# Low-rank attention with a gated feed-forward block: two early loads, the first batch's small pieces and one slot of batch 2 are moved

## The chip, the cores and the metric

The kernel runs on one core of a Trainium2 chip. The core has five engines that work side by side, each with its own queue of instructions taken in order: TensorE (PE in the profile, its weight loads PEld), VectorE (DVE), ScalarE (ACT), GpSimd (POOL) and SyncE (SP). Transfers are issued on the queues of SP, ACT and POOL and carried by 16 DMA engines that all of them share. TensorE reads SBUF and writes PSUM. Engines wait for one another on semaphores.

The metric is the device time of one execution in microseconds (us), less being better. It is given as the median of several runs.

## The reference

Part one is attention with keys and values that are projected from 1024 positions down to 64. There are 8 batches, 8 heads, 1024 positions and 64 elements per head. With E and F of 64 x 1024:

```
k_proj = E @ k          # per batch and head: 64 x 64
v_proj = F @ v
scores = (q @ k_proj.T) / 8
attn   = softmax(scores, over the 64 projected positions)
x      = attn @ v_proj  # heads side by side: 8192 tokens x 512
```

Part two is a gated feed-forward block on the 8192 tokens, with weights of 512 x 1536, 512 x 1536 and 1536 x 512:

```
g   = x @ w_gate
out = (g * sigmoid(g) * (x @ w_val)) @ w_out
```

## The kernel before, in words

Everything that TensorE multiplies is bf16. The weights stay in SBUF. The tokens are cut into 16 chunks (`c`) of 512: chunk c is half `ch` of batch `b`. For each chunk the feed-forward part goes over 12 blocks (`f`) of 128 columns. A block has a gate product (`f_g`, L367: four matmuls into a bank of PSUM called `gps`, then a tanh on ACT), a value product (`f_v`, L373: four matmuls into `vps`, then two operations on DVE that make the hidden tile `hT`), and a third of an output product of the chunk before (`f_y`, L386). These 192 blocks are the main loop. Every block t has two slots, 2t (between gate and value product) and 2t + 1 (after the output product), and the attention of later batches is laid into these slots by a table written out by hand (`place`, L426).

The attention of one batch has these pieces:

- `u_KV` (L140): k and v times E and F, giving the projected keys `ks` and values `BDV`. `u_V0` (L167) is the values' part for batch 0, a few head pairs at a time, with a copy by ACT.
- `u_KT` (L187): the projected keys transposed, and laid by four DVE copies into a block-diagonal operand `BD` for two positions at once.
- `u_T` (L211) transposes q on TensorE for chunks 0 and 1; `u_TD` (L226) has a DMA transpose do it for the others.
- `u_S` (L242): scores for one of eight units of a batch (chunk half, head group g, position pair i), four matmuls, then exp on ACT into `ee`. `u_R` (L263): row sums and reciprocals on DVE. `u_N` (L271): `ee` times the reciprocals, giving the bf16 attention tile `AA`.
- `u_A` (L289) transposes `AA` on TensorE, with a copy by DVE or ACT into `AT`; `u_AD` (L234) has a DMA transpose do it.
- `u_PV`, `u_PV2`, `u_PV1` (L305 to L343): attention times projected values, copied to `xT`, which is the operand of the feed-forward products.

For batches from 1 on, `u_S` of unit j stands in a slot `s0 + o + 3j`, `u_R` and `u_N` in the slot behind it, and the two `u_AD` four slots behind units 3 and 7. For batch 2, `o` is 13 and s0 is 48, so its first scores stand in slot 61, behind the output product of block 30. The transpose that they read, `u_TD(2, 0)`, is issued on SP in slot 57, once the load of q has landed.

The first half of chunk 0 has nothing to hide behind and is written out instruction by instruction (L459 to L570). The order of lines is the order of each engine's queue. ACT and SP issue the first loads: the first four heads of k in f32 (`kraw`, two loads, cast to bf16 by DVE and ACT), E and F. POOL makes the two identity matrices for transposes, then issues q, the other heads of k, v and the weights, which are cast to bf16 by the transfer itself. POOL can have eight loads under way; the ninth waits for the first to land. `warm` (L495) issues matmuls on zeros. `turn` transposes E and F. In the last lines, `f_mm` (L350) does the first half (256 tokens) of the products of blocks 0 and 1, between the pieces `u_A` and `u_PV2` that make the second half of `xT`; blocks 0 and 1 of the loop then do the second half, and from block 2 on the products have 512 tokens.

Of the kernel before, what the change touches and what calls it, by code (L numbers as in the profile page):

```python
# [22 lines left out]
P = 128  # L23
# [11 lines left out]
def kernel(  # L35
# [235 lines left out]
    def u_N(b, u):  # L271
        ch, w = divmod(u, 4)
        g, i = divmod(w, 2)
        if (b, ch) in BY_DMA:
            if (b, ch, "d") not in AA:
                AA[b, ch, "d"] = aw.tile([P, 4, H, KP], BF16, name="AAd", tag="AAd")
            a = AA[b, ch, "d"][:, 2 * i : 2 * i + 2, 4 * g : 4 * g + 4, :]
        else:
            a = AA[b, u] = aw.tile([P, 2, 4, KP], BF16, name="AA", tag="AA", bufs=4)
            a = a[:]  # L280
        eng = nc.vector if (b, u) == (0, 3) else nc.gpsimd
        eng.tensor_tensor(  # L282
            out=a.rearrange("p j h k -> p h j k"),
            in0=ee.pop((b, u))[:],
            in1=rr.pop((b, u))[:].unsqueeze(3).to_broadcast([P, 4, 2, KP]),
            op=ALU.mult,
        )
# [138 lines left out]
    def place(b):  # L426
        s0 = 48 * (b - 1)
        if b == 1:
            put(22, u_TD, 1, 0)
            put(29, u_KV, 1, "k")  # L430
            put(32, u_KT, 1)
            put(40, u_KV, 1, "v")
            sa = (35, 36, 37, 38, 41, 42, 43, 44)
            put(41, u_AD, 1, 0)
            put(30, u_TD, 1, 1)
            put(47, u_AD, 1, 1)
            sp = (44, 45, 46, 46, 66, 67, 68, 69)
        else:
            put(s0 + (8 if b == 2 else 0), u_KV, b)
            put(s0 + (11 if b == 2 else 3), u_KT, b)  # L440
            o = 13 if b == 2 else 6
            put(s0 + (9 if b == 2 else -6), u_TD, b, 0)
            put(s0 + (11 if b == 2 else -4), u_TD, b, 1)
            sa = [s0 + o + 3 * j for j in range(NJ)]
            put(sa[3] + 4, u_AD, b, 0)
            put(sa[7] + 4, u_AD, b, 1)
            sp = [s0 + i for i in (39, 41, 43, 45, 57, 59, 61, 63)]
        for j in range(NJ):
            put(sa[j], u_S, b, j)
            put(sa[j] + 1, u_R, b, j)  # L450
            put(sa[j] + 1, u_N, b, j)
        for i in range(8):
            put(sp[i], u_PV, b, i // 4, i % 4)
# [5 lines left out]
    with tc.manual_schedule():  # L459

        kb[0] = kv_pool.tile([P, H, NJ, D], BF16, name="kb", tag="kb")
        kraw = [aw.tile([P, 2, NJ * D], FP32, name="kraw", tag=tag) for tag in ("qTd", "AAd")]
        for i in range(2):
            nc.scalar.dma_start(
                out=kraw[i][:],
                in_=k[0, 2 * i : 2 * i + 2].rearrange("h (p j) d -> p h (j d)", j=NJ),
            )
        ef = []
        for which, src in (("E", E), ("F", F)):
            raw = const.tile([KP, S], FP32, name=f"{which}raw")  # L470
            (nc.sync if which == "E" else nc.scalar).dma_start(out=raw[:], in_=src)
            ef.append(raw)
        zeros = const.tile([P, CW], BF16, name="zeros")
        nc.vector.memset(zeros[:], 0.0)
        make_identity(nc, ident_fp[:])
        make_identity(nc, ident_bf[:])
        for i in range(2):
            nc.vector.memset(ks[i][64:P], 0.0)
            nc.vector.memset(BD[i][:], 0.0)
        nc.vector.memset(BDV[1][:], 0.0)  # L480

        def turn(which, at, halves=(0, 1)):
            for half in halves:
                ps = bank(at, [P, 4, KP], FP32, "efp")
                for i in range(4):
                    j = 4 * half + i
                    nc.tensor.transpose(
                        out=ps[:, i, :],
                        in_=ef[which][:, bass.ds(j, P, step=NJ)],
                        identity=ident_fp[:KP, :KP],  # L490
                    )
                js = slice(4 * half, 4 * half + 4)
                copy(nc.scalar, (ET, FT)[which][:, js, :], ps[:])

        def warm(n):  # L495

            ps = bank("v", [P, CW], FP32, "warm")
            for _ in range(n):
                nc.tensor.matmul(
                    out=ps[:], lhsT=zeros[:, 0:P], rhs=zeros[:],  # L500
                    start=True, stop=True,
                )


        dve, act = nc.vector, nc.scalar
        load_q(0, 0, (0, 2))
        load_k(0, 4, 8)
        load_q(0, 0, (2, 4))
        load_v(0, (0, 4, 6, 8))
        load_w_gv(0, 1)  # L510
        load_w_gv(1, 2, (0,))
        warm(11)
        turn(0, "v")
        warm(4)
        for h in range(4):
            for n in range(2):
                eng = act if (h, n) == (3, 1) else dve
                ds = slice(256 * n, 256 * (n + 1)) if h == 3 else slice(0, 512)
                if n == 0 or h == 3:
                    copy(eng, kb[0][:, h].rearrange("p j d -> p (j d)")[:, ds], kraw[h // 2][:, h % 2, ds])  # L520
        u_KV(0, "k", (0, 4), at="y")
        warm(1)
        u_T(0, 0, "a", act)
        u_KT(0, at="v", prs=(0, 2))
        u_T(0, 2, "a", act)
        turn(1, "a", (0,))
        u_S(0, 0, "g")
        u_R(0, 0)
        u_N(0, 0)
        load_w_gv(1, 2, (1,))  # L530
        warm(1)
        u_KV(0, "k", (4, 8), at="y")
        turn(1, "a", (1,))
        u_KT(0, at="v", prs=(2, 4))
        warm(1)
        u_T(0, 1, "a", act)
        u_A(0, 0, dve)
        u_T(0, 3, "a", dve)
        u_S(0, 2, "g")
        u_R(0, 2)  # L540
        u_N(0, 2)
        u_S(0, 1, "g")
        u_R(0, 1)
        u_N(0, 1)
        load_w_gv(2, 4)
        u_S(0, 3, "v")
        u_R(0, 3)
        u_V0(0, 2, "y")
        u_PV2(0, 0, 0, 0, act)
        warm(1)  # L550
        u_V0(2, 3, "y")
        u_A(0, 2, dve)
        u_PV1(0, 0, 2, 0, dve)
        u_V0(3, 4, "v")
        u_PV1(0, 0, 3, 0, act)
        u_N(0, 3)
        f_mm(0, 0, 0, 0)
        u_A(0, 1, act)
        u_A(0, 3, dve)
        f_mm(0, 0, 1, 0)  # L560
        u_PV2(0, 0, 0, 1, act)
        u_PV2(0, 0, 1, 1, dve)
        f_mm(0, 1, 0, 0)
        f_mm(0, 1, 1, 0)
        load_w_gv(4, 6)
        load_q(0, 1, hs=(0, 4))
        load_w_gv(6, 8)
        load_q(0, 1, hs=(4, 8))
        load_w_gv(8, 10)
        load_w_gv(10, 12)  # L570
        load_q(1, 0)
        load_k(1)
        load_wo(0)
        load_wo(1)

        for i, u in enumerate(range(4, 8)):
            put(11 + i, u_T, 0, u)
            put(13 + i, u_S, 0, u)
            put(14 + i, u_R, 0, u)
            put(14 + i, u_N, 0, u)  # L580
            put((17, 18, 20, 21)[i], u_A, 0, u, nc.scalar)
        put(19, u_PV, 0, 1, 0)
        put(20, u_PV, 0, 1, 1)
        put(22, u_PV, 0, 1, 2)
        put(22, u_PV, 0, 1, 3, nc.vector)
        put(20, load_v, 1)
        put(20, load_q, 1, 1)
        for b in range(1, B):
            place(b)
        for b in range(2, B):  # L590
            s0 = 48 * (b - 1) - (20 if b == 3 else 24)
            at = (43, 43, 44, 45) if b == 2 else (s0, s0 + 2, s0 + 4, s0 + 6)
            put(at[0], load_k, b)
            put(at[1], load_v, b)
            put(at[2], load_q, b, 0)
            put(at[3], load_q, b, 1)

        for s in slots:
            slots[s].sort(key=lambda x: x[0] not in (load_k, load_v, load_q))


        ypart = defaultdict(list)
        for c in range(B * CH - 1):
            for n in range(NFT):
                f = n if c else 4 + (2 * n + 1) // 3
                ypart[(c + 1) * NFT + f].append((c, n))

        for t in range(NIT):
            c, f = divmod(t, NFT)
            i = 1 if t < 2 else None  # L610
            f_g(c, f, i)
            run_slot(2 * t)
            f_v(c, f, i)
            for a in ypart.pop(t, ()):
                f_y(*a)
            run_slot(2 * t + 1)
        for n in range(9):
            f_y(B * CH - 1, n)
        f_y_last(B * CH - 1, 3)
        assert not slots and not ypart  # L620
# [29 lines left out]
```

The softmax here doesn't subtract the row's maximum and nothing guards it: scores larger than these inputs give would overflow.

## Time and profile before

| | us |
|---|---|
| time, median of 4 runs | 569.94 (569.52 to 570.31) |
| profiled execution: its time | 570.12 |
| profiled execution: its span | 568.3 |
| TensorE busy | 557.7 (98%) |
| DVE, ACT, POOL busy | 340.3, 235.6, 110.0 |
| q of chunk 0, first half: issued, landed | 1.77, 9.57 |
| kraw, second half: landed, first cast | 7.35, 7.40 |
| k, heads 4 to 7: landed, first matmul | 11.83, 11.92 |
| first gate matmul | 20.39 |
| first gate product with 512 tokens | 25.50 |
| S of batch 2, unit 0 | 105.07 |

The profile is of one execution. A line of its timeline has the start, the duration (or, for several merged instructions, the time that they cover), the engine, the source line, the operation with output and inputs, the shape, and in brackets how long the engine had stood idle and what released it. L138 is the line of a copy helper, so its groups are told apart by the tile they write. Busy time of TensorE is modelled at the end of each matmul; the starts of neighbouring matmuls tell more of its pace. A DMA view lists the queues: q0 is POOL's, q10 ACT's and q1 SP's in this run, with the packets, the MB and the share of the 16 engines' time. Bytes of q0 are counted as written (bf16), half of what it reads.

### The profile page before, as it was taken

What the parts mean: (1) busy time and instruction counts of PE and PEld (TensorE: products, weight loads), DVE (VectorE), ACT (ScalarE), POOL (GpSimd) and SP (SyncE); (2) the same over time, 40 slices, a digit from 0 to 9 for tenths busy, and PEclk for the clock granted to TensorE, in tenths of its full rate; (3) what the DMA queues carried; (4) which work ended last, traced back from release to release, by engine and by line L of the source; (5) the groups of instructions that cost most, each with busy time, mean ns of one, the idle gap of its engine ahead of it and who ended that gap; (6) DMA issues with size and microseconds to landing.
All of it is one profiled execution on the core that took longest, in us unless ns stands there. A gap on an engine that the chain in (4) does not pass through costs nothing.

```text
span 568.3 us, 7876 instructions
## 1 busy us (share of the span) xinstructions
PE 557.7 (98%) x2911; PEld 266.4 (47%) x2966; DVE 340.3 (60%) x580; ACT 235.6 (41%) x413; POOL 110.0 (19%) x123
## 2 busy tenths in 40 slices
PE   8899999999999999999999999999999999999997
PEld 4554444444444444444444444444444444444444
DVE  4686764766376654766466655666547665545550
ACT  3464442453435433443434434354343542443222
POOL 6751250124002400124002230023100220000000
PEclk9999999999999999999999999999999999999999
DMA  9999999729902696129930499105990214101012
GB/s 205 178 198 186 178 142 201 139 59 200 199 26 73 107 199 122 37 57 157 187 83 37 76 180 197 50 18 105 195 182 20 59 36 74 38 37 37 20 39 92
DMA packets 111159, 62.91 MB, mean 111 GB/s; under 512 B 64272, under 2 KB 102416, under 8 KB 111120
## 3 DMA queue, kind: packets, MB, share of 16 engines
q0 software_dynamic: 42816, 29.36, 35.9%
q1 hardware_dynamic: 67392, 31.46, 26.8%
q10 hardware_dynamic: 912, 1.57, 0.9%
q8 instruction: 23, 0.38, 0.3%
q14 instruction: 16, 0.13, 0.1%
HBM read 60.29 MB, written 16.78 MB: 136 GB/s over the span
## 4 chain that ended last, share of the span: by engine, by line
PE 94%; DMA 3%; ACT 1%; issue 1%; DVE 0%; POOL 0%; POOLq 0%
PE gps L358 29%; PE vps L358 29%; PE yps L396 28%; PE kvp L150 3%; PE sc L251 3%; PE pv L309 2%; DMA qb<-in_q_dram 1%; DMA qTd<-qb 1%; PE aTp L298 0%; ACT ee L255 0%; PE qTp L217 0%; ACT th L370 0%; POOL AA L282 0%; PE pv L324 0%; PE kTp L194 0%
## 5 line engine op out<-in xcount | busy, mean ns | idle before, releaser
L377 DVE SCALAR_TENSOR_TENSOR s<-th,gps 128x512 f32<-128x512 f32 x192 | 130.5, 680 | 135.6 <-ACT th L370 135.2
L358 PE MATMUL gps<-xT,wg 128*128 128x512 bf16 (+1 forms) x756 | 195.6, 377 | 1.3
L358 PE MATMUL vps<-xT,wv 128*128 128x512 bf16 (+1 forms) x763 | 196.2, 377 | 0.7
L396 PE MATMUL yps<-wo,hT 128*128 128x512 bf16 (+2 forms) x759 | 191.3, 376 | 0.8
L370 ACT ACTIVATE th<-gps 128x512 f32<-128x512 f32 x192 | 114.7, 597 | 155.6 <-PE gps L358 145.7
L382 DVE TENSOR_TENSOR hT<-s,vps 128x512 bf16<-128x512 f32 x192 | 132.0, 688 | 20.7 <-DVE s L377 0.9
L282 POOL TENSOR_TENSOR AAd<-ee,rr 128x512 bf16<-128x512 f32 x56 | 58.3, 1042 | 343.0 <-issue 156.4
L396 PEld LDWEIGHTS <-hT 128*128 128x128 bf16 x780 | 76.2, 98 | 89.9
L358 PEld LDWEIGHTS <-wv 128*128 128x128 bf16 x776 | 74.0, 98 | 83.2 <-issue 2.9
L358 PEld LDWEIGHTS <-wg 128*128 128x128 bf16 x776 | 74.1, 98 | 81.1 <-issue 1.0
L406 ACT ACTIVATE ysb<-yps 128x512 f32<-128x512 f32 (+1 forms) x65 | 38.4, 591 | 76.7 <-PE yps L396 71.3
L138 ACT CAST xT<-pv 128x512 bf16<-128x512 f32 (+1 forms) x62 | 35.9, 581 | 51.8 <-PE pv L309 50.5
L266 DVE TENSOR_REDUCE zz<-ee 128x8 f32<-128x512 f32 x64 | 43.5, 679 | 21.4 <-ACT ee L255 21.4
L255 ACT ACTIVATE ee<-sc 128x512 f32<-128x512 f32 x64 | 37.9, 595 | 24.8 <-PE sc L251 23.6
L251 PEld LDWEIGHTS <-qTd 128*128 128x128 bf16 x224 | 17.1, 98 | 13.9 <-DMA qTd<-qb 0.9
L309 PE MATMUL pv<-AT,BDV 128*128 128x512 bf16 x60 | 22.4, 379 | 0.2
L251 PE MATMUL sc<-BD,qTd 128*128 128x128 bf16 x224 | 21.7, 219 | 0.5 <-DMA qTd<-qb 0.4
L268 DVE RECIPROCAL rr<-zz 128x8 f32<-128x8 f32 x64 | 13.0, 203 | 6.3
L108 POOL DMA_DIRECT2D qb<-in_q_dram x18 | 16.3, 906 | 0.6 <-DMA qb<-in_q_dram 0.6
L150 PE MATMUL kvp<-kb,ET 128*64 128x512 bf16 (+1 forms) x72 | 15.5, 358 | 0.0
L162 DVE CAST BDV<-kvp 64x256 bf16<-64x256 f32 x7 | 3.0, 426 | 19.9 <-ACT ks L158 17.8
L150 PE MATMUL kvp<-vb,FT 128*64 128x512 bf16 x56 | 13.4, 382 | 0.0
(59 smaller groups left out, 136.4 us busy)
## 6 DMA issues: line engine op xcount, KB each, us to landing
out_dram<-ysb SPq DMA_DIRECT2D x63, 256.0 KB, 2.3
qb<-in_q_dram POOLq DMA_DIRECT2D x14, 512.0 KB, 18.1
kb<-in_k_dram POOLq DMA_DIRECT2D x7, 1024.0 KB, 11.4
vb<-in_v_dram POOLq DMA_DIRECT2D x7, 1024.0 KB, 13.9
wo<-in_moe_w_out_dram POOLq DMA_DIRECT2D x2, 768.0 KB, 22.2
wg<-in_moe_w_gate_dram POOLq DMA_DIRECT2D x5, 256.0 KB, 8.1
wv<-in_moe_w_val_dram POOLq DMA_DIRECT2D x5, 256.0 KB, 8.7
kraw<-in_k_dram ACTq DMA_DIRECT2D x2, 512.0 KB, 5.0
```

The source lines that it names most:

```text
L138: (nc.scalar.copy if eng is nc.scalar else eng.tensor_copy)(out=out, in_=in_)
L150: nc.tensor.matmul(out=t[lo : lo + 64, h0:h1].rearrange("p h d -> p (h d)"), lhsT=w[:, j, :], rhs=src[b][:, h0:h1, j, :], start=(j == 0), ...
L251: nc.tensor.matmul(out=ps[:, n, :], lhsT=t[:, n, :], rhs=BD[b % 2][:, 4 * g + n, :], start=True, stop=True)
L255: nc.scalar.activation(out=e[:].rearrange("p h j k -> p (h j k)"), in_=ps[:].rearrange("p a k -> p (a k)"), func=AF.Exp, scale=scale,)
L266: nc.vector.reduce_sum(out=z[:], in_=e[:], axis=AX.X)
L282: eng.tensor_tensor(out=a.rearrange("p j h k -> p h j k"), in0=ee.pop((b, u))[:], in1=rr.pop((b, u))[:].unsqueeze(3).to_broadcast([P, 4, 2 ...
L358: nc.tensor.matmul(out=ps[:, ts], lhsT=(wg, wv)[w][:, kt, f * P : (f + 1) * P], rhs=x[:, kt, ts], start=(kt == 0), stop=(kt == NKT - 1),)
L370: nc.scalar.activation(out=th[:], in_=ps[:], func=AF.Tanh, scale=0.5)
L377: nc.vector.scalar_tensor_tensor(out=s1[:], in0=th[:], scalar=1.0, in1=g[:], op0=ALU.add, op1=ALU.mult)
L382: nc.vector.tensor_tensor(out=hT[c][:, f, :], in0=s1[:], in1=ps[:], op=ALU.mult)
L396: nc.tensor.matmul(out=yy[c][:, cs], lhsT=hT[c][:, f, i * P : (i + 1) * P], rhs=wo[:, f, cs], start=(f == 0), stop=(f == NFT - 1),)
L406: nc.scalar.activation(out=ysb[:, cs], in_=yy[c][:, cs], func=AF.Copy, scale=0.5)
```

## The change

Three things move; no operation is added or taken away.

First, the loads of q (first half of chunk 0's first half) and of k (heads 4 to 7) are issued on POOL ahead of the identity matrices. The memsets of DVE for `ks`, `BD` and `BDV`, all at the start before, are put at four places later on, except that of `ks[0]`.

Second, pieces of batch 0. `u_N(0, 3)` goes from DVE to POOL. `u_V0(3, 4)` comes ahead of `u_PV1` of pair 2. `u_A(0, 1)` comes ahead of the first `f_mm`, with its copy on DVE, and `u_A(0, 3)` between the first gate and value products, with its copy on ACT. The two `u_PV2` of the second half swap their copying engines, and the second comes one product later. The load of gate weights of columns 2 and 3 is issued behind `u_N(0, 0)`, that of the value weights behind `u_N(0, 3)`.

Third, the offset `o` of batch 2 is 14 instead of 13: its eight `u_S`, `u_R`, `u_N` and both `u_AD` come one slot later.

```diff
-        eng = nc.vector if (b, u) == (0, 3) else nc.gpsimd
-        eng.tensor_tensor(
+        nc.gpsimd.tensor_tensor(
...
-            o = 13 if b == 2 else 6
+            o = 14 if b == 2 else 6
...
+        load_q(0, 0, (0, 2))
+        load_k(0, 4, 8)
         zeros = const.tile([P, CW], BF16, name="zeros")
         nc.vector.memset(zeros[:], 0.0)
         make_identity(nc, ident_fp[:])
         make_identity(nc, ident_bf[:])
-        for i in range(2):
-            nc.vector.memset(ks[i][64:P], 0.0)
-            nc.vector.memset(BD[i][:], 0.0)
-        nc.vector.memset(BDV[1][:], 0.0)
+        nc.vector.memset(ks[0][64:P], 0.0)
...
-        load_q(0, 0, (0, 2))
-        load_k(0, 4, 8)
         load_q(0, 0, (2, 4))
...
+        nc.vector.memset(BD[0][:], 0.0)
         u_KV(0, "k", (0, 4), at="y")
...
         u_R(0, 0)
+        nc.vector.memset(ks[1][64:P], 0.0)
         u_N(0, 0)
         load_w_gv(1, 2, (1,))
+        load_w_gv(2, 4, (0,))
...
         u_N(0, 1)
-        load_w_gv(2, 4)
         u_S(0, 3, "v")
...
         u_A(0, 2, dve)
+        u_V0(3, 4, "v")
         u_PV1(0, 0, 2, 0, dve)
-        u_V0(3, 4, "v")
         u_PV1(0, 0, 3, 0, act)
         u_N(0, 3)
+        load_w_gv(2, 4, (1,))
+        u_A(0, 1, dve)
         f_mm(0, 0, 0, 0)
-        u_A(0, 1, act)
-        u_A(0, 3, dve)
+        u_A(0, 3, act)
         f_mm(0, 0, 1, 0)
-        u_PV2(0, 0, 0, 1, act)
-        u_PV2(0, 0, 1, 1, dve)
+        u_PV2(0, 0, 0, 1, dve)
         f_mm(0, 1, 0, 0)
+        u_PV2(0, 0, 1, 1, act)
         f_mm(0, 1, 1, 0)
+        nc.vector.memset(BD[1][:], 0.0)
+        nc.vector.memset(BDV[1][:], 0.0)
```

## The prediction

> **What bounds the kernel now.** First I read the page's busy times and the chain that ended last.
>
> ```profile
> PE 557.7 (98%) x2911; PEld 266.4 (47%) x2966; DVE 340.3 (60%) x580; ACT 235.6 (41%) x413; POOL 110.0 (19%) x123
> ...
> PE 94%; DMA 3%; ACT 1%; issue 1%; DVE 0%; POOL 0%; POOLq 0%
> ```
>
> TensorE is the bound, and nothing in this change removes a matrix instruction. A gain can only come from time in which TensorE stands still. Starts of neighbouring matmuls in the trace are 0.216 us apart in the loop (four cost 0.86). There is one true hole after 26 us, and the rest lies ahead of 25.5 us. So I read the timeline of TensorE there, first the hole:
>
> ```profile
> 102.76 1.03 PE L358 MATMUL vps<-xT,wv 128*128 128x512 bf16 x4
> 103.62 1.03 PE L396 MATMUL yps<-wo,hT 128*128 128x512 bf16 x4
> 105.07 0.40 PE L251 MATMUL sc<-BD,qTd 128*128 128x128 bf16 x4 [0.41 <-DMA qTd<-qb]
> ```
>
> S of batch 2, unit 0, was ready to be issued at 103.62 + 0.86 = 104.48 and came at 105.07: 0.59 lost, to a transpose that was issued at 98.16 and landed 6.86 later, at 105.02. Then the start, in the timeline of TensorE (start, duration, idle before and its releaser):
>
> ```profile
> 18.30 0.40 PE L298 MATMUL aTp<-ident_bf,AA 128*128 128x128 bf16 x4
> 19.21 0.27 PE L336 MATMUL pv<-AT,BDV 128*128 128x256 bf16 x1 [0.52 <-DVE AT L138]
> 19.32 0.22 PE L170 MATMUL kvp<-zeros 128*128 128x128 bf16 x1
> 19.47 0.44 PE L178 MATMUL kvp<-vb,FT 128*64 128x64 bf16 x16
> 20.27 0.28 PE L336 MATMUL pv<-AT,BDV 128*128 128x256 bf16 x1 [0.36 <-ACT BDV L185]
> 20.39 0.89 PE L358 MATMUL gps<-xT,wg 128*128 128x256 bf16 x4
> 21.12 0.61 PE L298 MATMUL aTp<-ident_bf,AA 128*128 128x128 bf16 x8
> 21.57 0.60 PE L358 MATMUL vps<-xT,wv 128*128 128x256 bf16 x4
> 22.18 0.60 PE L324 MATMUL pv<-AT,BDV 128*128 128x256 bf16 x4
> 22.62 0.60 PE L358 MATMUL gps<-xT,wg 128*128 128x256 bf16 x4
> ```
>
> TensorE waits for DVE's copy of A(0,2), then for the last piece of V, then inside the first gate product for the copy of its fourth operand. Last, the queues, because two loads move. The DMA view of 2.0 to 6.3 us and then of 6.3 to 9.6 us:
>
> ```profile
> q10 hardware_dynamic: 538, 1.07, 75.9%
> q1 hardware_dynamic: 80, 0.26, 22.3%
> ```
> ```profile
> q0 software_dynamic: 1206, 0.43, 112.8%
> q10 hardware_dynamic: 86, 0.24, 32.6%
> ```
>
> POOL's queue (q0) has its first load issued at 1.77, yet moves nothing before 6.3: until then ACT's and SP's loads (kraw, E, F) fill the engines. From then on POOL's loads land one behind another: q at 9.57, k at 11.83, v from 15.86 to 18.4, gate weights of column 0 at 19.17, of column 1 at 21.75 (issued 9.85, landing 11.9 later), value weights of column 1 at 21.9.
>
> **The change part by part.**
>
> *q and k loads ahead of the identity.* POOL issues q at 0.74 instead of 1.77 and k at 1.80 instead of 2.83; the four identity instructions (1.03 us) follow, and end at about 3.6 instead of 1.8. Their readers come at 6.00 (turn of E) and 9.61 (transpose of q): hidden, and without that cover 1.8 us. The third load (q, second half) goes out at 3.6 as before. The direct gain is T(0,0): its wait for q ended at 9.57, while the warm matmul ahead of it, issued at 9.11, was over by 9.50, so 0.11 at most. The indirect one is that q0's whole train, the weights at its end included, may come earlier. Lower bound 0 (q0 stays behind the hardware loads), upper bound 1.03 (all of the earlier issue). The rows: 1.8 to 6.3 us ran at 296 GB/s, 6.3 to 7.5 at 222, and later q0 alone at 193 written, which is 386 read, since it casts f32 to bf16. So the window 6.3 to 7.5 has room for 1.2 x (1 - 222/386) = 0.5 us of q0's work; q0 will fill part of it. I take 0.3.
>
> The Trainium skill, "DMA: Bandwidth & Descriptors", section Queues, rings and completion order, says that each engine goes round robin over its queues packet by packet. This speaks against the change, because kraw's second half would then share with q; the rows above, with none of q0's packets before 6.3, do not show such sharing at the start. By the page alone I would let kraw's second half come 1.0 later (an estimate); the third gate matmul below would start at 22.72 + 1.0 - 0.11 = 23.61, the tail's gain would shrink to 0.10, and the sum would be 569.25.
>
> *Memsets.* DVE's five at the start become one (ks[0], 0.27) and four are spread out. BD[0] (0.48) falls behind kraw's casts (8.03 to 8.5; DVE idles until 10.11), ks[1] (0.27) between a reciprocal that ends at 13.28 and a copy at 13.73, BD[1] and BDV[1] (0.75 together) behind DVE's last copy, where DVE idled 1.25 ahead of L377. Zero; without the gaps 0.48, 0.27 and 0.75 would be late in turn for the two KT copies and for s.
>
> *V0(3,4) ahead of PV1, A and PV2 rearranged, N(0,3) on POOL.* Step by step. A(0,2) is issued by 18.53; V0(3,4) now fills the wait: zeros 18.54, its 16 matmuls 18.69 to 19.13 (0.44), for which v has landed at 18.4. ACT copies 19.17 to 19.44 (0.04 and 0.27 as at 19.95). PV1 of pair 2 stays at 19.21, pair 3 at 19.49 instead of 20.27; its copy (0.32 later, 0.37 long) ends 20.18, and the fourth gate matmul starts at 20.23 instead of 21.02.
>
> N on POOL takes 1035 ns against 682 on DVE, but starts at 19.17 instead of 19.86 and ends at 20.20 instead of 20.54. A(0,1) is issued 19.62 to 19.84, copied by DVE by 20.46; A(0,3) at 20.34, copied by ACT (0.59) by 21.36; value product 20.56 to 21.00; PV2 of the first pair 21.00 to 21.22. The Trainium skill, "GPSIMD Engine Reference", section Engine selection, gives such an operation to VectorE, as GpSimd is about 2x slower. The rows here say 1.52x; by the page's 2x N would end at 20.53, A(0,3) 0.19 later, and the sum would stay, behind the wait that follows.
>
> What is late next: the gate weights of column 1, landed at 21.75, are wanted at 21.22. Unmoved, they hold the product until 21.80, then it takes 0.44, PV2 of the second pair starts at 22.24, and its copy is ready 1.06 later (22.18 to 22.60, 0.59 of ACT, 0.05): the third matmul of the full gate product at 23.30 instead of 23.71, a gain of 0.41. With weights 0.58 earlier there is no wait: 21.22 to 21.66, third matmul at 22.72, a gain of 0.99. With the 0.3 above: 0.71. T(0,0)'s 0.11 only counts if that wait is gone.
>
> *Weight loads.* The gate half of columns 2 to 4 goes out at about 15.2 instead of 19.13, in time that POOL idled (15.24 to 17.13). N(0,3) then pushes the value half from 19.93 to 20.20 and the loads queued behind it on POOL by as much. Cover: the train has one load less in front; landings against first use were 25.33 to 26.14, 26.86 to 28.95, 28.29 to 29.8. Zero; the narrowest margin is 0.8.
>
> *Batch 2's S one slot later.* The slot moves S, R, N and both AT transposes of batch 2. S(2,0) now stands behind four more gate matmuls, 104.48 + 0.86 = 105.34, after the landing at 105.02: the whole 0.59 goes. On SP the AT transposes come about 1.4 later: the first 122.26 + 1.4 + 4.4 = 128.1 against its reader at 141.40, the second 138.70 + 1.4 + 11.8 = 151.9 against 167.86. Behind that one on SP queues the qTd transpose of batch 3 at 145.65, 0.4 later at most, read at 163.3. Zero for these. On POOL the loads of batch 3 stand first in their slots and do not move.
>
> **Sum.** 0.71 + 0.59 = 1.30 off the span of 568.3, so 567.0. The profiled run took 570.12 (1.8 around its span), 0.18 above the median of 569.94; against the median 569.94 - 1.30 = 568.64. From the bounds: least 0.41 + 0.41 (the idle as printed) = 0.82, most 0.99 + 0.11 + 0.59 = 1.69, so 568.25 to 569.12.
>
> **Rivals.**
>
> *Landing does not move with the engines.* If S(2,0)'s transpose lands at 105.02 of the old clock, the two gains don't add: only one gate product (0.86) is done before it. 569.08. For it: that landing hangs on the load of q, issued 79.08 and landed 98.08, through crowded queues. Against it: q0 had been idle for ten microseconds before 76.26, so those loads start with the program's position.
>
> *The start gives nothing.* Another early load or copy turns up late, and only S's 0.59 is left: 569.35. For it: all weights are within 2 us of their use. Against it: all of them come from one train that moves forward too.
>
> *The other side: q and k go in front of kraw's second half.* The casts at 7.40 wait for that landing (7.35); what is late there shifts KV, KT, S, N. From TensorE's own path, the third gate matmul at 22.72 would need 0.99 of delay to lose the tail's gain and 1.58 to lose all; with 0.11 from T(0,0) the break-even is kraw 1.69 late. Whole q ahead (its stream took about 1.5, 7.5 to 9.0): just under break-even. q and k ahead (k landed 2.26 after q): 3.76 late, 569.94 + 2.07 = 572.0. For it: an isolated load of POOL, issued 76.26, moved its first packets about 2.1 later; from 0.74 that gives 2.9, while kraw's second half runs from 4.3. Against it: the hardware loads are all issued by 2.3, and at 3.9, when q could have begun, it did not get in.
>
> **How the numbers follow.** The measurement tells about 0.2% (1.14 us) from no change. Main case 0.62, seven eighths of it above 1.14 of gain: 0.54 faster, 0.08 same. Landing fixed 0.14 and start without gain 0.12: same. kraw pushed back 0.12: 0.10 slower, 0.02 same. Together faster 0.54, same 0.36, slower 0.10. The range from 568.0 (most gain, and the 0.3 by which the four runs differ from their median) to 569.7 (the case of S alone, with the same 0.3) leaves out the slower tenth and some of the main case.
>
> **What the profile would show.** Right: q0's packets start between 5.5 and 6.5, the casts of kraw still at 7.4, V0(3,4) before PV1 without the 0.52 and 0.36 of wait, a new wait of gate matmuls for wg near 21.3, the full gate stream from about 24.8 instead of 25.50, and no wait of L251 for qTd. Wrong: casts of kraw at 8 or later, the wait for wg as long as 0.6, or L251 waiting for qTd again.

## The result, and the profile after

The changed kernel takes 569.23 us (median of 34 runs, 568.85 to 570.70) against 570.07 for the kernel before (52 runs, 569.26 to 572.40). The ratio is 0.9984, with a 95% interval from 0.9980 to 0.9989: 0.91 us less, between 0.63 and 1.14. The gain is real, smaller than the 1.30 that was forecast, and it lies inside the 0.2% (1.14 us) that the forecast took as its border of "faster".

The page of the changed kernel, with the same three lines as were shown of before:

```profile
span 567.3 us, 7879 instructions
...
PE 556.8 (98%) x2911; PEld 266.3 (47%) x2966; DVE 339.9 (60%) x579; ACT 235.3 (41%) x413; POOL 111.0 (20%) x124
...
PE 93%; DMA 3%; POOL 1%; issue 1%; ACT 0%; DVE 0%; POOLq 0%
```

TensorE has the same 2911 matrix instructions and is still the bound. The span went from 568.35 to 567.28, by 1.07, so idle time of TensorE went away. First the place where half of the forecast lay, S of batch 2, in the timeline of TensorE (start, time covered, engine, line, operation, and in brackets the idle time and its releaser):

```profile
103.15 1.03 PE L395 MATMUL yps<-wo,hT 128*128 128x512 bf16 x4
104.01 1.03 PE L357 MATMUL gps<-xT,wg 128*128 128x512 bf16 x4
104.88 0.39 PE L251 MATMUL sc<-BD,qTd 128*128 128x128 bf16 x4
```

The wait of 0.41 (0.59 by the starts) is gone. The gate product stands in front of S and covers the transpose, which landed at 104.32. (Landings here and below are mostly the issue plus the time to landing, which a view gives to a tenth of a microsecond, so they are good to 0.05.) Next the end of the hand-written start, in the same view:

```profile
18.32 0.40 PE L297 MATMUL aTp<-ident_bf,AA 128*128 128x128 bf16 x4
18.56 0.22 PE L170 MATMUL kvp<-zeros 128*128 128x128 bf16 x1
18.71 0.44 PE L178 MATMUL kvp<-vb,FT 128*64 128x64 bf16 x16
19.24 0.56 PE L335 MATMUL pv<-AT,BDV 128*128 128x256 bf16 x2
19.63 0.39 PE L297 MATMUL aTp<-ident_bf,AA 128*128 128x128 bf16 x4
19.85 0.67 PE L357 MATMUL gps<-xT,wg 128*128 128x256 bf16 x4
20.36 0.38 PE L297 MATMUL aTp<-ident_bf,AA 128*128 128x128 bf16 x4
20.58 0.60 PE L357 MATMUL vps<-xT,wv 128*128 128x256 bf16 x4
21.02 0.38 PE L323 MATMUL pv<-AT,BDV 128*128 128x256 bf16 x2
21.24 0.60 PE L357 MATMUL gps<-xT,wg 128*128 128x256 bf16 x4
...
24.52 1.02 PE L357 MATMUL gps<-xT,wg 128*128 128x512 bf16 x3
```

V0 fills the time of the copy, both PV1 stand together, and the waits of 0.52 and 0.36 are gone. The gate weights of column 1, feared late at 21.75, landed at 20.67, so the line at 21.24 has no wait. The first gate product with 512 tokens, the last line, starts at 24.52 instead of 25.50: 0.98 gained.

A place that the prediction does not mention takes half of this back. It is ten microseconds further on, where T (L217) of unit 6 needs heads 4 to 7 of q for chunk 1:

```profile
32.73 1.03 PE L357 MATMUL vps<-xT,wv 128*128 128x512 bf16 x4
33.59 0.39 PE L251 MATMUL sc<-BD,qT 128*128 128x128 bf16 x4
34.31 0.40 PE L217 MATMUL qTp<-ident_bf,qb 128*128 128x128 bf16 x4 [0.34 <-DMA qb<-in_q_dram]
34.55 1.03 PE L357 MATMUL gps<-xT,wg 128*128 128x512 bf16 x3
```

T was ready to go at 33.59 + 4 x 0.055 = 33.81 and came at 34.31: 0.50 lost. In the kernel before, the first gate product with 512 tokens and the same T are these lines:

```profile
25.50 1.02 PE L358 MATMUL gps<-xT,wg 128*128 128x512 bf16 x3
...
34.80 0.39 PE L217 MATMUL qTp<-ident_bf,qb 128*128 128x128 bf16 x4
```

There T came at 34.80 and its q had landed at 33.62, so 1.18 was to spare. The program is now 0.98 earlier there, and the load landed 0.69 later: 1.18 - 0.98 - 0.69 = -0.49.

| place on TensorE | before | after | so far |
|---|---|---|---|
| first gate product with 512 tokens | 25.50 | 24.52 | -0.98 |
| first output product, behind T's wait of 0.50 | 57.24 | 56.77 | -0.47 |
| behind S of batch 2, whose wait of 0.59 is gone | | | -1.06 |
| span | 568.35 | 567.28 | -1.07 |

Last the queues from 2.0 to 6.3 us (queue: packets, MB, share of the 16 engines) and the first load on POOL:

```profile
q10 hardware_dynamic: 523, 1.03, 74.0%
q1 hardware_dynamic: 80, 0.26, 22.3%
q0 software_dynamic: 22, 0.01, 1.3%
```
```profile
1.25 1.06 POOL L108 DMA_DIRECT2D qb<-in_q_dram  x1 [0.80 <-POOLq L635]
```

POOL begins q at 1.25, not at the 0.74 that the prediction used. Its queue moves 22 packets before 6.3, where it had none. The third load (q, second half) goes out at 4.11 instead of 3.58, where the prediction left it at 3.6. The loads land when they did: q 9.55 (9.57 before), k 11.91 (11.83), kraw's second half 7.25 (7.35), the weights of column 0 19.16 (19.17).

### The profile page after: what moved, and what is told of

It is laid out like the page before. It is cut to its first block, busy times and chain, and to the rows that moved or that the text cites. A ratio compares the mean times of both kernels' runs of the same rounds, so it can differ in the third digit from the quotient of the medians.

```text
span 567.3 us, 7879 instructions
## 1 busy us (share of the span) xinstructions
PE 556.8 (98%) x2911; PEld 266.3 (47%) x2966; DVE 339.9 (60%) x579; ACT 235.3 (41%) x413; POOL 111.0 (20%) x124
## 4 chain that ended last, share of the span: by engine, by line
PE 93%; DMA 3%; POOL 1%; issue 1%; ACT 0%; DVE 0%; POOLq 0%
PE yps L395 29%; PE vps L357 28%; PE gps L357 28%; DMA qb<-in_q_dram 3%; PE kvp L150 3%; PE sc L251 2%; PE pv L308 2%; POOL AA L281 1%; POOL wv L118 0%; POOL wg L118 0%; PE qTp L217 0%; PE aTp L297 0%; PE kTp L194 0%; POOL qb L108 0%; DVE zz L266 0%
## 5 line engine op out<-in xcount | busy, mean ns | idle before, releaser
L251 PEld LDWEIGHTS <-qTd 128*128 128x128 bf16 x224 | 17.2, 98 | 13.2
L251 PE MATMUL sc<-BD,qTd 128*128 128x128 bf16 x224 | 21.6, 219 | 0.1
```

Of the source, the lines that this page charges most:

```text
L251: nc.tensor.matmul(out=ps[:, n, :], lhsT=t[:, n, :], rhs=BD[b % 2][:, 4 * g + n, :], start=True, stop=True)
```

## The experiments

The theory at this point: the slot of S is worth 0.59; the regrouped start is worth up to 0.98, of which the late q takes 0.50; the early loads and memsets are worth nothing. Against it stood that the early loads carry the gain of the start, that the landing of S's transpose is fixed in time, and that T's wait has another origin than the earlier program. For the late q, and for the gate weights of column 1 (21.75 before, 20.67 after), which cannot hang on loads that land as before, a cause was looked for in the queues.

**The three parts alone.** First the slot, put into the kernel before:

```diff
-            o = 13 if b == 2 else 6
+            o = 14 if b == 2 else 6
```

> The kernel before with one edit, the offset of batch 2 at 14. My theory: S of batch 2, unit 0, no longer waits for its transpose; the whole 0.59 us goes and nothing else moves: span 567.7, ratio 0.9990, first full gate product still at 25.50. Rival: the landing of the transpose, or a reader further on, comes later by as much; then the gain is under 0.2 us.

Measured: 569.64 us, ratio 0.9995 (0.9987 to 1.0004). The span of the profiled execution is 567.72, 0.63 under before's. The timeline of TensorE:

```profile
104.46 1.03 PE L358 MATMUL gps<-xT,wg 128*128 128x512 bf16 x4
105.32 0.39 PE L251 MATMUL sc<-BD,qTd 128*128 128x128 bf16 x4
```

No wait is left, with the transpose landed at 104.83. The start is that of before (full gate product at 25.47). The path shows the 0.59; the times hold it, but cannot tell it from nothing.

Then the early loads and the memsets alone, put into the kernel before:

```diff
+        load_q(0, 0, (0, 2))
+        load_k(0, 4, 8)
         zeros = const.tile([P, CW], BF16, name="zeros")
...
-        for i in range(2):
-            nc.vector.memset(ks[i][64:P], 0.0)
-            nc.vector.memset(BD[i][:], 0.0)
-        nc.vector.memset(BDV[1][:], 0.0)
+        nc.vector.memset(ks[0][64:P], 0.0)
...
-        load_q(0, 0, (0, 2))
-        load_k(0, 4, 8)
```

> The kernel before with the q and k loads ahead of the identity and the memsets spread out, and nothing else. My theory after seeing the changed kernel's trace: the first load of POOL starts only at 1.25 and its bytes pass the hardware loads no earlier than before; q lands at 9.55, k at 11.9, column 1's gate weights where the instruction fetch lets them; time unchanged within 0.15 us. Rival (my prediction's step): the train of weights comes 0.3 us earlier and the start gains about that much.

Measured: 569.82 us, ratio 0.9998 (0.9988 to 1.0009), no difference. Its one profiled execution has a span of 567.49, which would mislead by itself: in that execution kraw's second half landed at 6.94, and S of batch 2 came at 104.22 without a wait, its transpose having landed at 104.15. The landing of kraw's second half was 6.95 to 7.35 in the three profiles without early loads and 6.94 to 7.75 in the eleven with them. One execution varies by more than this part is worth.

The regrouped start alone (the pieces of V0, PV1, N, A and PV2 and the two weight loads, as in the changed kernel, nothing else):

```diff
         u_A(0, 2, dve)
+        u_V0(3, 4, "v")
         u_PV1(0, 0, 2, 0, dve)
-        u_V0(3, 4, "v")
         u_PV1(0, 0, 3, 0, act)
         u_N(0, 3)
+        load_w_gv(2, 4, (1,))
+        u_A(0, 1, dve)
         f_mm(0, 0, 0, 0)
-        u_A(0, 1, act)
-        u_A(0, 3, dve)
+        u_A(0, 3, act)
...
```

> The kernel before with the pieces of V, A, N, P V and the weight loads regrouped; identity, memsets and batch 2 as before. My theory: the first full gate product comes at 24.5 instead of 25.5 if column 1's gate weights land at 20.7, and at 25.1 if they land at 21.7; which of the two depends on whether TensorE's 16 KB instruction fetch at about 19.7 takes a DMA engine just ahead of their packets. If 24.5, the transpose of unit 6 then waits about 0.5 us for q near 33.8. The loop keeps the 0.59 of batch 2. Span 567.7 to 567.9. Rival: the early loads are what brought the weights forward; then they land at 21.7 here in any case, and the full gate product is at 25.1.

Measured: 569.68 us, ratio 0.9992 (0.9983 to 1.0001), span 568.23. Its start gained 0.76 (full gate product at 24.74), with column 1's weights landing at 21.45. The timeline of TensorE and then the list of its waits (engine, tile, line, releaser: us in total, times, longest):

```profile
21.46 0.61 PE L357 MATMUL gps<-xT,wg 128*128 128x256 bf16 x4 [0.28 <-DMA wg<-in_moe_w_gate_dram]
```
```profile
PE sc L251 <- DMA qTd<-qb: 0.8, 1, 0.8
...
PE gps L357 <- DMA wg<-in_moe_w_gate_dram: 0.3, 1, 0.3
```

So the wait for the gate weights that the prediction put near 21.3 exists, in this execution. And without the later slot S of batch 2 waits 0.8 (0.98 by the starts): its transpose landed at 104.96. The regrouping alone is given back there almost whole in this execution (0.76 - 0.24 at T of unit 6 - 0.39 more wait at S = 0.13, against 0.12 by the spans). The span of 567.7 to 567.9 that was expected was missed: it counted on a wait of 0.59 there. So in this execution the regrouping needed the later slot. The times do not show it: the three parts alone give 0.28, 0.11 and 0.46, each with an interval that takes in 0, and their sum of 0.85 is close to the 0.91 of the whole.

**The late q.** In the changed kernel, T, S, R and N of units 6 and 7 were put one slot later:

```diff
-            put(11 + i, u_T, 0, u)
-            put(13 + i, u_S, 0, u)
-            put(14 + i, u_R, 0, u)
-            put(14 + i, u_N, 0, u)
+            i6 = i + (i > 1)
+            put(11 + i6, u_T, 0, u)
+            put(13 + i6, u_S, 0, u)
+            put(14 + i6, u_R, 0, u)
+            put(14 + i6, u_N, 0, u)
```

> The changed kernel with T, S, R and N of units 6 and 7 of batch 0 one slot later, so that the transpose of unit 6 is wanted 0.86 us later. My theory: the wait for q near 33.8 us (0.50 between the starts of neighbouring matmuls) is a real loss and goes whole: span 566.8. Rival: it only hides another late piece (exp, N or A of units 6 and 7, or another load), and the time stays at 567.3.

Measured: 569.20 us, ratio 0.9987 (0.9978 to 0.9996), span 566.80. The timeline of TensorE:

```profile
33.83 1.03 PE L357 MATMUL gps<-xT,wg 128*128 128x512 bf16 x4
34.70 0.39 PE L251 MATMUL sc<-BD,qT 128*128 128x128 bf16 x4
34.92 0.39 PE L217 MATMUL qTp<-ident_bf,qb 128*128 128x128 bf16 x4
```

T stands at 34.92 and its q had landed at 33.93. The wait is gone, the first output product starts at 56.28 instead of 56.77, and the span is 0.48 shorter than the changed kernel's: the 0.50 at T was on the path to the end of the profiled execution. The time of 569.20 cannot be told from the changed kernel's 569.23.

Why did q land late? It was issued at 24.61, only 0.29 later than before, but landed 0.69 later, 2.13 behind the load ahead of it (value weights of columns 6 and 7) instead of 1.33. In that gap the DMA view from 32.0 to 32.2 us shows a second queue:

```profile
q0 software_dynamic: 77, 0.04, 140.8%
q8 instruction: 1, 0.02, 29.5%
```

q8 is instruction fetch. The page lists 23 packets of 16 KB on it, against 5877 matmuls and weight loads of TensorE, one for about 256. The share of 29.5% of 16 engines over 0.2 us is 0.94 us on one engine. While it runs, POOL's queue carries less: 135.1% from 32.2 to 32.9 us, against 147.7% from 33.2 to 33.9. A load has landed when its last engine is done, so the idea is that a fetch at the wrong moment holds up one sixteenth of a load, and so all of it. Two runs were to move the fetch. The first takes three zero matmuls from the changed kernel's start:

```diff
-        warm(11)
+        warm(8)
```

> The changed kernel with 8 instead of 11 zero matmuls at the very start, where TensorE has idle time before E lands. It takes 6 instructions out of TensorE's stream, so the second 16 KB instruction fetch comes about 0.65 us later (32.7 instead of 32.1). In the six profiles so far q for unit 6 landed late (33.9 to 34.3) in the three with that fetch at 32.15 or earlier, and at 33.5 to 33.6 in the three with it at 32.56 or later. My theory: it lands at 33.5, the transpose of unit 6 does not wait, span 566.8. Rival: the load is late because POOL issues it 0.3 us later; then it lands at 34.3 again and the span is 567.3.

Measured: 570.53 us, ratio 1.0015 (1.0006 to 1.0024), span 569.5. This missed its aim, for another reason: everything came later by 1.3, the loads behind the start as well, and q was late again (35.76, with a wait of 0.64 at T), and S of batch 1 waited 0.58 for its transpose. What the start looked like is told in the last section. Its q load was late with a fetch close to the landing ahead of it, as in the other late cases, but the fetch was not moved away as planned, so the run does not test the idea.

The second cuts the same zero matmuls into more instructions, so that the fetch comes earlier and the work stays the same:

```diff
-        def warm(n):
+        def warm(n, w=CW):
...
-                    out=ps[:], lhsT=zeros[:, 0:P], rhs=zeros[:],
+                    out=ps[:, 0:w], lhsT=zeros[:, 0:P], rhs=zeros[:, 0:w],
...
-        warm(4)
+        warm(8, CW // 2)
```

> The changed kernel with four zero matmuls of 512 columns cut into eight of 256: the same time, 8 more instructions of TensorE, so both fetches come earlier by 0.2 to 0.45 us. My theory: the first fetch now stands ahead of column 1's gate weights; they land at 21.5 to 21.8 instead of 20.7, the first full gate product comes at about 24.9 instead of 24.5; the transpose of unit 6 is then wanted when q lands (34.3), so its wait goes and the end hardly moves, span 567.2 to 567.4. Rival: the fetch has nothing to do with these landings; 20.7, 24.5 and a wait of 0.5 as in the changed kernel.

Measured: 568.99 us, ratio 0.9989 (0.9981 to 0.9998), span 566.85. The timeline of TensorE:

```profile
33.53 0.39 PE L251 MATMUL sc<-BD,qT 128*128 128x128 bf16 x4
33.76 0.39 PE L217 MATMUL qTp<-ident_bf,qb 128*128 128x128 bf16 x4
33.99 1.03 PE L357 MATMUL gps<-xT,wg 128*128 128x512 bf16 x3
```

The second fetch started at 31.04 instead of 32.08, q landed at 33.68, 1.33 behind the load ahead of it, and T does not wait. The first fetch went from 19.77 to 18.25, further than counted on, and met another load: the value weights of column 0 came 1.77 behind the gate weights (0.73 in the changed kernel), and their product waited 0.15. All profiles of this study side by side, with the start of the second fetch, the landing of the load ahead of q, that of q (heads 4 to 7 of chunk 1), and the gap between the two:

| profile | fetch | ahead of q | q | gap | fetch minus ahead |
|---|---|---|---|---|---|
| before | 32.76 | 32.29 | 33.62 | 1.33 | +0.47 |
| after | 32.08 | 32.18 | 34.31 | 2.13 | -0.10 |
| slot alone | 33.24 | 32.29 | 33.53 | 1.24 | +0.95 |
| early loads alone | 32.56 | 32.26 | 33.59 | 1.33 | +0.30 |
| regrouping alone | 32.15 | 32.24 | 34.27 | 2.03 | -0.09 |
| units 6, 7 later | 31.77 | 32.10 | 33.93 | 1.83 | -0.33 |
| three zeros fewer | 33.23 | 33.42 | 35.76 | 2.34 | -0.19 |
| zeros halved | 31.04 | 32.35 | 33.68 | 1.33 | -1.31 |
| V0 late | 32.92 | 32.55 | 33.99 | 1.44 | +0.37 |
| changed, second | 32.03 | 32.12 | 34.15 | 2.03 | -0.09 |
| changed, third | 33.76 | 33.89 | 36.03 | 2.14 | -0.13 |
| units 6, 7 later, second | 32.33 | 32.23 | 34.37 | 2.14 | +0.10 |
| N(0,3) on DVE | 32.08 | 31.30 | 32.63 | 1.33 | +0.78 |
| slot 61 | 32.03 | 31.92 | 34.25 | 2.33 | +0.11 |

The gap is 1.83 or more in all eight profiles in which the fetch began between 0.33 ahead of that landing and 0.11 behind it, and at most 1.44 in the six others. The rival that POOL's later issue delays q falls: the regrouping alone issued it at 24.37 and it was late, the halved zeros at 24.38 and V0 late at 24.69, and there it was not. In the five profiles where the fetch began 0.30 to 0.95 behind the landing, the load behind q was the late one instead: it came 1.45 to 1.96 behind q, against 1.34 with the halved zeros. That the program's own position decides this, by way of the fetch, is well supported for this load; that the fetch's packet sits in front of q's on one engine was not seen packet by packet and stays the explanation that fits.

It is not a rule for every load. With the halved zeros the fetch at 31.04 began 0.08 behind the landing of the gate weights of columns 6 and 7 (30.96), and the value weights behind them came 1.38 later, which is not late.

For the gate weights of column 1 the idea is left open. They came 1.73 to 2.11 behind the load ahead of them in eight profiles, with the first fetch from 0.40 ahead of that landing to 0.06 behind it. They came 0.70 to 0.82 behind it in five, where the fetch began 0.18 to 1.02 behind that landing in three, but 0.12 and 0.04 ahead of it in two (the changed kernel among them). Those two lie inside the other band, so the fetch alone does not sort them.

**The parts of the regrouping.** First, in the changed kernel, V0(3,4) was put back behind PV1 of pair 2:

```diff
         u_A(0, 2, dve)
-        u_V0(3, 4, "v")
         u_PV1(0, 0, 2, 0, dve)
+        u_V0(3, 4, "v")
         u_PV1(0, 0, 3, 0, act)
```

> The changed kernel with the last piece of V back behind the P V product of pair 2. My theory: the fourth gate matmul is back at 21.0, the first full gate product at about 25.3 instead of 24.5; the transpose of unit 6 no longer waits, which gives back 0.5: span 567.6. Rival: the other pieces (A and N) carry the gain; then the full gate product stays below 24.8.

Measured: 569.43 us, ratio 0.9993 (0.9984 to 1.0002), span 567.65. The timeline of TensorE:

```profile
19.32 0.27 PE L335 MATMUL pv<-AT,BDV 128*128 128x256 bf16 x1 [0.52 <-DVE AT L138]
...
20.38 0.28 PE L335 MATMUL pv<-AT,BDV 128*128 128x256 bf16 x1 [0.36 <-ACT BDV L185]
...
20.72 0.67 PE L357 MATMUL gps<-xT,wg 128*128 128x256 bf16 x4
```

Both waits are back as they were, and the full gate product starts at 25.38, 0.86 later than with the change. This one line is most of the gain of the start. The end came only 0.37 later, since T of unit 6 does not wait now.

Then N(0,3) was put back on DVE:

```diff
-        nc.gpsimd.tensor_tensor(
+        eng = nc.vector if (b, u) == (0, 3) else nc.gpsimd
+        eng.tensor_tensor(
```

> The changed kernel with N of unit 3 back on DVE. My theory: A of unit 3 is ready 0.34 us later and DVE's copy of A of unit 1 0.6 later, so the first full gate product comes at about 24.9 instead of 24.5; POOL's loads go out 1.0 earlier, but their train is full and q for unit 6 still lands after 33.4, so most of the 0.4 is given back by the shorter wait there: span 567.2 to 567.5. Rival: DVE is free enough, and the full gate product stays at 24.5.

Measured: 569.24 us, ratio 0.9989 (0.9980 to 0.9997), span 567.16. A(0,3) came at 20.56 after 0.26 of waiting, column 1's weights landed at 21.62, and the full gate product started at 24.92. But the loads of the main loop came a microsecond sooner (q at 32.63), so T does not wait, and the end is the same. The lines from the value product on:

```profile
20.80 0.60 PE L358 MATMUL vps<-xT,wv 128*128 128x256 bf16 x4
21.23 0.38 PE L324 MATMUL pv<-AT,BDV 128*128 128x256 bf16 x2
21.63 0.61 PE L358 MATMUL gps<-xT,wg 128*128 128x256 bf16 x4
```

The value product is 0.22 later than with the change. The gate product was due 0.66 behind it, as there, at 21.46, and column 1's weights held it for another 0.17. So of the 0.40 at the full gate product, 0.22 belong to N; the load had been issued before N ran, and why it came late is open as above. On this path 0.40 at the start and 0.50 at T trade places.

Last, the slot alone was undone in the changed kernel:

```diff
-            o = 14 if b == 2 else 6
+            o = 13 if b == 2 else 6
```

> The changed kernel with batch 2's offset back at 13. My theory: S of batch 2, unit 0, would be ready at 104.0, its transpose lands at 104.3 to 104.9, so the wait is back with 0.3 to 0.9 us: span 567.5 to 568.1. Rival: the earlier start has given the transpose enough room, no wait, span 567.2.

Measured: 569.49 us, ratio 0.9994 (0.9985 to 1.0004), span 567.80. The timeline of TensorE:

```profile
103.11 1.03 PE L395 MATMUL yps<-wo,hT 128*128 128x512 bf16 x4
104.51 0.40 PE L251 MATMUL sc<-BD,qTd 128*128 128x128 bf16 x4 [0.37 <-DMA qTd<-qb]
```

The wait is back, 0.53 by the starts (0.59 before). The landing, 104.47 here, was at 105.02 before: it moved forward with the program. It varies, too: issue to landing took 6.4 to 7.5 over the fourteen profiles. The start of this execution differs as well (column 1's weights at 21.49, full gate product at 24.82, a wait of 0.16 at T), so the wait at S is compared here and not the span.

**Repeats.** The changed kernel as it is, beside the two runs on the fetch:

> The changed kernel once more, on the chip of the three others, to compare with them. My theory: first full gate product 24.5 if column 1's gate weights land at 20.7 and 24.9 if at 21.7; unit 6 waits for q only in the first case; span 567.3 either way within 0.2.

Measured: 569.14 us, ratio 0.9991 (0.9982 to 1.0000), span 567.14; the full gate product at 24.48, column 1's weights at 20.43, and T waits 0.40. And once more, on another chip, together with the version that has units 6 and 7 one slot later:

> The changed kernel, on the chip of the three others, as their yardstick: span 567.2 within 0.2, the transpose of unit 6 waiting 0.3 to 0.5 us for q near 33.8.

Measured: 569.33 us, ratio 0.9990 (0.9981 to 0.9999). Its one profiled execution took 571.01, the longest of its twelve, with a start of the kind that the last section describes (kraw's second half landed at 7.75); T waits 0.61 in it.

> Units 6 and 7 one slot later, beside the changed kernel on one chip. My theory: the wait for q near 33.8 goes in the timed runs as in the profile; 0.3 to 0.5 us under the changed kernel beside it. Rival: the profile showed an unlucky execution of the changed kernel and the timed runs rarely wait; then the two are within 0.15 us.

Measured: 569.23 us, ratio 0.9983 (0.9975 to 0.9992), span 567.46. The timeline of TensorE:

```profile
21.91 0.61 PE L357 MATMUL gps<-xT,wg 128*128 128x256 bf16 x4 [0.34 <-DMA wg<-in_moe_w_gate_dram]
...
25.20 0.38 PE L357 MATMUL gps<-xT,wg 128*128 128x512 bf16 x1
```

T again does not wait, but column 1's weights landed at 21.84 this time and cost 0.50 (0.34 as printed). It is 0.10 under the changed kernel on the same chip, and the intervals overlap. The 0.3 to 0.5 that was expected was missed, and the rival's 0.15 held; whether the timed runs of the changed kernel rarely wait at T, or this version lost elsewhere what it gained there, the times do not tell. Whether it is a better version stays open, and so does the gain of every part alone whose interval takes in 1.

## Why the prediction was right or wrong

The forecast time of 568.64 is 0.59 under the median of 569.23, which lies inside the range of 568.0 to 569.7. The direction is right, and so are the two places. The size was 1.30 against 0.91 (0.63 to 1.14). By the sign chances, 0.54 went to a gain above 0.2% and 0.36 to one below; the measured centre belongs to the second, with the interval's end on the border. That the sum came this close is in part luck: in the profiled execution the start gave 0.27 more than its term, and a wait that the prediction does not have took 0.50 away.

- **S of batch 2, 0.59: right.** No L251 wait for its transpose is left, neither with the slot alone nor with the whole change, and 0.53 comes back when the slot is undone.
- **The start, 0.71: the mechanism is right, the size and its reason are not.** The steps came true within 0.03: V0's zeros at 18.56 (forecast 18.54), PV1 at 19.24 (19.21), A(0,3) at 20.36 (20.34), the value product at 20.58 (20.56) and the gate product of column 1 at 21.24 (21.22). V0 in the gap takes both waits away, and 0.86 hangs on that line. The profiled execution gained 0.98, the upper bound without T(0,0)'s 0.11. Where column 1's weights were late, as in the regrouping alone, 21.45 still held the product for 0.44 (0.28 printed). From the first gate product to the full stream it took 4.66 and 4.67 where nothing waited (4.82 with the halved zeros and their wait of 0.15), and 5.01 to 5.17 in the four profiles where a product waited for column 1's weights. So the upper bound of 0.99 occurs, and late weights leave 0.48 to 0.64 of it, a little over the lower bound of 0.41. The middle was chosen with "I take 0.3", from loads issued sooner. That step failed: q issued 0.52 sooner landed no sooner (9.55 and 9.57, each good to 0.05), and the early loads alone changed nothing. Column 1's weights did come 1.08 sooner, but not by a train that moves forward: column 0's weights ahead of them kept their time.
- **"Zero; the narrowest margin is 0.8": the step that failed.** It gave the margins of three loads of weights (columns 2 to 5) and left out q of chunk 1, which travels in the same train and is read by T of unit 6. The margin of 1.18 there would have outlasted a gain of 0.98 alone; the load landing 0.69 later used it up, and 0.50 was lost. The rival "the start gives nothing" had the sentence for it, "Another early load or copy turns up late", but priced it as the loss of all that the start gains.
- **The early loads.** T(0,0)'s 0.11 did not show: T started at 9.63, q having landed at 9.55. The rival that puts q and k ahead of kraw's second half fell too: kraw landed at 7.25 and its reader was not late. The round robin that the Trainium skill, "DMA: Bandwidth & Descriptors", section Queues, rings and completion order, describes would by the prediction's estimate have made it 1.0 later; 22 packets of POOL's queue against 603 of ACT's and SP's from 2.0 to 6.3 us do not show it.
- **The rival of a landing that stays where it is fell.** Before, the transpose landed at 105.02, and after at 104.32. The prediction's "0.4 later at most" for the transpose of batch 3 was too little: with the slot alone it was issued at 146.97 instead of 145.65. It landed at 154.7 and was read 8 us later, so nothing came of it.
- **N(0,3) on POOL and the memsets.** The first gives 0.22 at the value product, and nothing at the end of the profiled execution; the memsets, with the early loads, show no cost.

The sum by the runs: 0.98 - 0.50 + 0.59 = 1.07 for the profiled execution. The times give 0.91, and 1.07 lies inside their interval; which waits the executions without a profile had is not known.

## What to carry to other kernels

When a stretch of work moves forward, list every load that is read behind it, up to the next point where something is known to have slack, and set each landing against the new time of its reader; a margin equal to the gain is none. A gain at one place is only kept if the next late thing moves along: of the 0.76 that the regrouping alone gained at the start, its profiled execution lost 0.24 at T and 0.39 at S. Parts worth 0.1% are read from the path of several executions, since one execution's span can differ by more for reasons that have nothing to do with the edit.

## What the runs showed of the hardware

**Instruction fetch takes part in the traffic.** A fetch of 16 KB holds one DMA engine for about 0.9 us, and the q load of the table landed 0.4 to 1.1 later when a fetch began close to the landing ahead of it; another load, with a fetch as close to the landing ahead of it, was not late (value weights of columns 6 and 7, with the halved zeros). Adding eight half-size matmuls in place of four moved both fetches, and with them the landing of loads that nobody touched.

**The pace of TensorE at the start hangs on little.** The timeline of TensorE for the kernel with three zero matmuls fewer:

```profile
6.14 1.11 PE L485 MATMUL efp<-ident_fp,Eraw 64*128 64x64 f32 x8 [1.35 <-DMA Eraw<-in_E_dram]
7.28 1.86 PE L497 MATMUL warm<-zeros 128*128 128x512 bf16 x4
```

And for the changed kernel:

```profile
5.99 1.06 PE L485 MATMUL efp<-ident_fp,Eraw 64*128 64x64 f32 x8 [0.73 <-DMA Eraw<-in_E_dram]
7.08 1.02 PE L497 MATMUL warm<-zeros 128*128 128x512 bf16 x4
```

The same four zero matmuls take 1.86 instead of 1.02, and the pace stays at about half until 10.7. On the same chip three zero matmuls fewer cost 1.39 us (569.14 for the changed kernel, 570.53). The first zero matmuls of every run stand 0.43 apart, the half pace, and later ones 0.21 or 0.22. With eleven of them the full pace was there by the four at about 7.1 in twelve profiles; with eight it came only near 10.7.

The changed kernel itself had a half-pace start in one of its profiled executions, by another way: its zero matmuls were 0.22 apart from 4.09 on, TensorE was idle for 1.18 ahead of E, and the next four took 1.84. The rows by window of that execution (window, length, busy time of TensorE, its weight loads, DVE, ACT and POOL, the granted clock, share and GB/s of the DMA engines) show the clock halved for about 3.4 us:

```profile
4.00:7.40 3.40, 2.20 (x14) 1.36 (x13) 0.84 (x2) 0.37 (x1) 3.40 (x6) 1.00 1.20 266
7.40:10.90 3.50, 3.50 (x12) 1.62 (x11) 1.17 (x3) 0.78 (x2) 1.87 (x3) 0.51 1.46 186
10.90:12.00 1.10, 1.10 (x13) 0.74 (x13) 0.24 (x1) 0.75 (x2) 0.23 (x1) 1.00 1.53 186
```

For the kernel with three fewer the same view prints 1.00 throughout, but it does so for the first zero matmuls of every run too, so at the start a printed 1.00 tells nothing of the pace. The Trainium skill, "TensorE: Matmul & The Clock Gate", Part 1: The HAM clock gate, says that the array runs at half rate until it was busy for a window of about 3.4 us that runs freely, and drops back after an idle window of that length. The length agrees with the rows, and a free window agrees with the same kernel starting in both ways. That the window must be idle does not agree: in the 3.40 us ahead of the drop TensorE was busy for 2.20, with 2.26 between the zero matmuls (5.12 to 7.38) and the turn of E inside them. In the execution that kept its pace the same stretch was 1.82 (5.26 to 7.08). How much idle time in a window is enough was not measured.

**A load issued sooner need not arrive sooner.** POOL's first load begins at 1.25, 0.80 after its last instruction before it, and its queue moves almost nothing until near 6.2 us. By then E has landed (5.9); kraw's second half (7.25) and F (9.1) are still under way. Issued 0.52 sooner than before, the load landed at the same time (9.55 and 9.57).
